# Reordering filler blocks, transposes and scores inside the attention slots of a global-local attention and routed-MLP kernel

## The chip, the cores and the metric

The kernel runs on one core of one Trainium2 chip. TensorE (PE) multiplies matrices into PSUM; VectorE (DVE) and ScalarE (ACT) read PSUM and work on SBUF; GpSimd (POOL) works on SBUF; POOL, ACT and SyncE (SP) issue DMAs. The metric is the time of one execution on the device in microseconds (us); lower is better. Several runs are taken and the median is given.

## The reference: what is computed

Two stages. The first is attention for 8 batches, 8 heads, 512 local and 32 global tokens of 64 values. Local tokens attend to the 32 global keys and to local keys no more than 32 places away; global tokens attend to all 544 keys.

```python
s_g = scale * np.matmul(q_g, k_all.transpose(0, 1, 3, 2))
out_g = np.matmul(sm(s_g), v_all)
mask = np.abs(pos[:, None] - pos[None, :]) <= window
s_ll = np.where(mask, scale * np.matmul(q_l, k_l.transpose(0, 1, 3, 2)), -1000000000.0)
s_l = np.concatenate([s_lg, s_ll], axis=-1)
out_l = np.matmul(sm(s_l), np.concatenate([v_g, v_l], axis=2))
```

The 4352 x 512 result `x` goes through 8 experts that are all evaluated and weighted by a matrix P, made by eight rounds of row and column scaling:

```python
for e in range(E):
    h = np.maximum(x @ w1[e], 0.0)
    out += P[:, e:e + 1] * (h @ w2[e])
```

## The kernel before

The order of instructions on each engine is the order in which the program text emits them; each engine works through its own list in order, and semaphores hold an instruction until its inputs and its buffer are ready.

The attention part runs in slots. Slot `s` belongs to a pair of heads of one batch (32 pairs, 4 per batch). It works on two pairs at once: it makes the scores of pair `s` and finishes pair `s-1`. The steps, by function and profile line:

- `st_B(s, part)`: scores on PE (L301 against local keys, L303 against global keys) for three, three and two blocks of 64 queries; for each block DVE applies mask and maximum (L308, tile `ms`) and ACT the exponential with its sum (L311, tile `Pu`).
- `st_N(s)`: DVE takes reciprocals (L347) and normalises the local probabilities in two pieces, six blocks and two (L348); POOL normalises the part that belongs to global keys, shared by all queries (L352, tile `Pl`).
- `st_D1(s-1)`: eight PE transposes of the local probabilities (L359, tile `ptw`) and their copy to SBUF on DVE (L361, `pw`).
- `st_D2(s-1)`: two PE transposes of the shared ones (L367) and their copy on ACT (L369, `pg`).
- `st_A(s+1)`: eight PE transposes of keys and queries of the next pair (L275), copied by DVE (L276, `kTe`) and ACT (L285, `qbd`).
- `st_E(s-1)`: the outputs of the local queries (L380, L383), copied by ACT (L386; by DVE for pairs 4 to 7).
- Global queries are taken for two pairs at a time. `st_G0` gathers them on POOL (L399). `st_G1`, at the end of odd slots from the ninth on, makes their scores on PE (L409), the maximum on DVE (L411, L412) and the exponential on ACT (L414, `Pg`). In the slot after, `st_GN` normalises on DVE (L420, L421), `st_G2` makes five PE transposes (L428) and a copy on ACT (L430, `pgs`, one buffer), and `st_G3` the outputs on PE (L442, L443), copied by ACT (L447).

PSUM pools set part of the order: `ps_tr` has two buffers for all transposes, `ps_sc` two for scores and global outputs, `ps_po` one, shared by `st_E` and `st_G1`, and `ps_mm` two for fillers and logits.

A filler block fills PE between these steps: `p_l1` makes 128 rows of a hidden layer of one of the first four experts for one batch, with four matmuls of 512 columns (L468) into a `ps_mm` buffer. Its ReLU, which empties the buffer, is done by ACT (L471) or DVE (L473); every eighth block stores a finished tile (L475). `f1("av")` emits two blocks, the first emptied by ACT ("a"), the second by DVE ("v"). There are 288 blocks. Before the change slots 9 to 32 emit seven blocks (odd) or eight (even); those left at the end of the loop are emitted between the rounds of the scaling of P. Every fourth slot from 5 on also emits the routing logits (L455).

In slots from the ninth on, the order of PE's work before the change is: local transposes, two fillers, first scores, shared transposes, global transposes (even slots, and slot 9), second scores, two fillers, key and query transposes, third scores, a filler, outputs, global outputs (even slots, and slot 9), two fillers, then one more filler in even slots, and the logits and global scores where the slot has them. After the loop come the scaling rounds with the remaining fillers, and a long stage of the other experts and all second layers (L821, L839, L932).

In the code `s` is the slot, `HP` is 4, `NU` is 32, `g1` says that the slot ends with global scores, `g23` that the slot before it did.

Of the kernel before, what the change touches and what calls it, by code (L numbers as in the profile page):

```python
# [23 lines left out]
def kernel(  # L24
# [26 lines left out]
    HP = H // 2  # L51
# [40 lines left out]
    with tc.tile_pool(name="att_c", bufs=1) as att_c, \  # L92
# [106 lines left out]
        def cast_g(f, g):  # L199
            t = att_in.tile([P, NJ, 4, Dh], FP16, tag="gs", name="gs", bufs=3)  # L200
            r = B * GP
            nc.gpsimd.tensor_copy(out=t[0:r], in_=f[0:r, 4 * g : 4 * g + 4].rearrange("p h (s d) -> p s h d", s=NJ))
            return t
# [83 lines left out]
        def st_B(n, part):  # L287
            b, hp = divmod(n, HP)
            qb, kt = qbd[n % 2], kTe[n % NK]
            if part == 0:  # L290
                st[n] = dict(Pu=att_wk.tile([P, NHB, SW], FP16, tag="Pu", name="Pu"),
                             mx=att_wk.tile([P, NHB], FP32, tag="mx", name="mx"),
                             sm=att_wk.tile([P, NHB], FP32, tag="sm", name="sm"))
            d = st[n]
            i0 = 3 * part
            ni = min(3, NHB - i0)
            sc = ps_sc.tile([P, 512], FP32, tag="sc")
            ms = att_wk.tile([P, 3, SW], FP32, tag="ms")
            for ii in range(ni):
                i = i0 + ii  # L300
                nc.tensor.matmul(sc[:, SW * ii : SW * ii + KW], qb[:, i, :],  # L301
                                 kt[:, HB * i : HB * i + KW], start=True, stop=True)
                nc.tensor.matmul(sc[:, SW * ii + KW : SW * (ii + 1)], qb[:, i, :],  # L303
                                 kgT[:, hp, Sg * b : Sg * (b + 1)], start=True, stop=True)
            for ii in range(ni):
                i = i0 + ii
                mi = 0 if i == 0 else (2 if i == NHB - 1 else 1)
                nc.vector.tensor_tensor_reduce(  # L308
                    out=ms[:, ii, :], in0=sc[:, SW * ii : SW * (ii + 1)], in1=mask[:, mi, :],
                    scale=-scale, scalar=BIG, op0=ALU.add, op1=ALU.min, accum_out=d["mx"][:, i : i + 1])  # L310
                nc.scalar.activation(out=d["Pu"][:, i, :], in_=ms[:, ii, :], func=AF.Exp, scale=-1.0,  # L311
                                     bias=d["mx"][:, i : i + 1], accum_out=d["sm"][:, i : i + 1])
# [42 lines left out]
        def st_D1(n):  # L355
            d = st[n]
            ptw = ps_tr.tile([P, NHB, P], FP16, tag="tr")
            for i in range(NHB):
                nc.tensor.transpose(ptw[:, i, :], d["Pu"][:, i, 0:KW], identity)  # L359
            d["pw"] = att_wk.tile([P, NHB, P], FP16, tag="pw", name="pw")  # L360
            nc.vector.tensor_copy(out=d["pw"], in_=ptw)  # L361

        def st_D2(n):
            d = st[n]
            pt = ps_tr.tile([P, 2, P], FP16, tag="tr")
            for t in range(2):
                nc.tensor.transpose(pt[:, t, :], d["Pl"][:, 4 * t : 4 * t + 4, :], identity)  # L367
            d["pg"] = att_wk.tile([P, 2, P], FP16, tag="pg", name="pg")
            nc.scalar.copy(out=d["pg"], in_=pt)  # L369
# [53 lines left out]
        def st_G2(b, g):  # L423
            Pg = gs[(b, g)][0]
            pt = ps_tr.tile([P, 5, P], FP16, tag="tr")
            for t in range(5):
                c0 = P * t if t < 4 else S - P
                nc.tensor.transpose(pt[:, t, :], Pg[:, c0 : c0 + P], identity)  # L428
            pgs = att_wk.tile([P, 5, P], FP16, tag="pgs", bufs=1)
            nc.scalar.copy(out=pgs, in_=pt)  # L430
            gs[(b, g)] = pgs
# [29 lines left out]
        def p_l1(e, m, fm, eng, pool=None, tag="mm"):  # L461
            n = groups[m][1]
            if fm == 0:
                hTs[(e, m)] = hpool.tile([P, FT, n], FP16, tag="hT", name="hT")
            hT = hTs[(e, m)]
            ph = (pool or ps_mm).tile([P, 512], FP32, tag=tag, name="ph")
            for dk in range(DP):
                nc.tensor.matmul(ph[:, 0:n], wts[e][:, dk, P * fm : P * (fm + 1)], xT[m][:, dk, :],  # L468
                                 start=(dk == 0), stop=(dk == DP - 1))
            if eng == "a":  # L470
                nc.scalar.activation(out=hT[:, fm, 0:n], in_=ph[:, 0:n], func=AF.Relu)  # L471
            else:
                nc.vector.tensor_scalar(out=hT[:, fm, 0:n], in0=ph[:, 0:n], scalar1=0.0, scalar2=None, op0=ALU.max)  # L473
            if fm == FT - 1:
                (nc.scalar if pool else nc.sync).dma_start(out=hd[e][m], in_=hT)  # L475
# [14 lines left out]
        def f1(engs, **kw):  # L490
            nonlocal n1
            v = 0
            for eng in engs:
                k, fm = divmod(n1, FT)
                if k < len(fill) and slot >= HP * fill[k][1] + 5:
                    p_l1(*fill[k], fm, eng, **kw)
                    n1 += 1
                    v += 1 if fill[k][1] < B else 0.5
            return v
# [88 lines left out]
        for s in range(HP, NU + 1):  # L588
            slot = s
            b, hp = divmod(s, HP)  # L590
            g1 = s in gat
            g23 = s - 1 in gat
            if g1:
                gn = divmod(gat[s], 2)
            if g23:
                gp = divmod(gat[s - 1], 2)
            if s == HP:
                st_A(s + 1)
                st_B(s, 2)
                st_E(s - 1)  # L600
                st_N(s, 0, 6)
                st_N(s, 6, NHB)
                select_v(1, 0, (0, 1))
                st_B(s + 1, 0)
                select_v(1, 0, (2, 3))
                select_v(1, 1, (NJ - 1,))
                slot = s + 1
                va, vb = vab[1]
                nc.scalar.dma_start(out=vb[0:HB, 0 : NJ - 1], in_=va[HB:P, 0 : NJ - 1])
                nc.scalar.dma_start(out=vb[HB:P, 0 : NJ - 1], in_=va[0:HB, 1:NJ])  # L610
                cast_qk(1, 1, gq)
                gcast = [(cast_g(x[0], x[1]), x) for x in ((kgf, 1, kgT), (qgf, 0, qgT), (qgf, 1, qgT))]
                load_w1e(3)
            else:
                if HP + 1 < s <= 2 * HP:
                    st_B(s, 0)
                st_D1(s - 1)
                if g23:
                    st_GN(*gp)
            if g1 and s > HP + 1:  # L620
                st_G0(*gn)
            f1("aa")
            if 2 * HP < s < NU:
                st_B(s, 0)
            if s > HP:
                st_D2(s - 1)
            if g23:
                st_G2(*gp)
            if HP < s < NU:
                st_B(s, 1)  # L630
            if s > HP:
                f1("va")
            if HP < s < NU - 1:
                st_A(s + 1)
            if HP < s < NU:
                st_B(s, 2)
            if s > HP:
                f1("v")
                st_E(s - 1)
            if s == HP + 1:  # L640
                for t, (src, g, dst) in gcast:
                    transpose_g(t, g, dst)
                st_G0(*gn)
            if g23:
                st_G3(*gp)
            if s > HP:
                f1("va")
            if HP < s < NU:
                st_N(s, 0, 6)
                st_N(s, 6, NHB)  # L650
            if s > 2 * HP and not g1:
                f1("v")
            if s >= 5 and (s - 5) % HP == 0:
                logits(NJ * ((s - 5) // HP), NJ)
            if g1:
                st_G1(*gn)
            if s < NU and b + 1 < B:
                if hp == 0:
                    load_qk(b + 1, 0, (nc.sync, nc.sync))
                    load_qk(b + 1, 1, (nc.sync, nc.sync))  # L660
                elif hp == 1:
                    cast_qk(b + 1, 0, gq)
                    if b >= NL - 1:
                        load_w1d(b + 1)
                elif hp == 2:
                    vq = load_v(b + 1)
                    run(vq[:3])
                    cast_qk(b + 1, 1, gq)
                else:
                    run(vq[3:])  # L670
# [408 lines left out]
    for i, (m, e) in enumerate(units):  # L1079
# [9 lines left out]
        elif i % 2 == 0:  # L1089
# [45 lines left out]
            else:  # L1135
                n = groups[m][1]
                h = hs[i + 1]
                s = ss[i + 1] = xsp.tile([P, HF, n], FP16, tag="xs", name="sl")
# [96 lines left out]
```

## Time and profile before

| | us |
|---|---|
| median of three runs | 1045.23 (1043.06 to 1045.32) |
| the profiled execution, its time | 1043.48 |
| the profiled execution, its span | 1041.5 |
| PE busy | 1012.5 (97%) |
| DVE busy | 895.7 (86%) |
| ACT busy | 525.2 (50%) |
| the chain that ended last: share of PE | 79% |

The span runs from the first to the last instruction of the profiled execution. Busy time of PE counts a matmul until its modelled end, while the next one has begun, so short waits of PE are seen better in the starts of the timeline than in its busy share. In the view of waits a line reads: the instruction that waited, what it waited for, microseconds in total, how often, and the longest. In the timeline a line is start, length, engine, line of the kernel, operation, tiles, shape and how many were merged into it; idle time before it stands in brackets.

### The profile page before, as it was taken

The page shows a single profiled execution, that of the slowest core. Times are in us where ns is not written, and L with a number is a line of the kernel's source. Part 1 is how long each engine was busy: PE and PEld are TensorE (multiplying, and loading weights), DVE is VectorE, ACT ScalarE, POOL GpSimd, SP SyncE. Part 2 cuts the span into 40 slices and gives each one's busy share as a digit, 9 for nine tenths or more (in the row PEclk, how much of TensorE's full clock was granted, in tenths as well). Part 3 has the DMA queues.
Part 4 walks back from the last instruction along what each step waited for, and adds up shares of the span by engine and source line. Part 5 has one row for each costly group of instructions (what it writes and reads, how often), then busy time and mean ns, then how long its engine had stood idle before and what let it go on. Part 6 is the DMA issues. An engine that isn't in the chain of part 4 may idle for free.

```text
span 1041.5 us, 23189 instructions
## 1 busy us (share of the span) xinstructions
PE 1012.5 (97%) x9286; PEld 740.6 (71%) x9286; DVE 895.7 (86%) x1748; ACT 525.2 (50%) x1320; POOL 146.2 (14%) x237
## 2 busy tenths in 40 slices
PE   7899999999999999999999999999999999999998
PEld 4555555555555466777778878878878878878887
DVE  8687777777776786999898999999999999999986
ACT  7777888787876665223223333334334333333331
POOL 7441423424312102001100000000000000000000
PEclk9899999999999999999999999999999999999999
DMA  9887588989945989936866646556555555645651
GB/s 273 183 219 206 117 269 180 221 234 185 246 144 135 276 258 321 289 102 214 312 252 228 221 143 232 189 177 227 195 180 185 210 175 209 216 172 180 210 191 28
DMA packets 103499, 213.72 MB, mean 205 GB/s; under 512 B 34192, under 2 KB 68448, under 8 KB 92896
## 3 DMA queue, kind: packets, MB, share of 16 engines
q1 hardware_dynamic: 56928, 167.47, 46.3%
q0 software_dynamic: 43856, 35.14, 18.7%
q10 hardware_dynamic: 2608, 9.64, 2.4%
q8 instruction: 73, 1.20, 0.4%
q14 instruction: 34, 0.28, 0.1%
HBM read 174.41 MB, written 59.12 MB: 224 GB/s over the span
## 4 chain that ended last, share of the span: by engine, by line
PE 79%; DVE 10%; ACT 6%; issue 2%; DMA 1%; SPq 0%; POOL 0%; ACTq 0%; DVEq 0%
PE m L932 26%; PE ph L468 15%; PE pf L839 10%; PE pm L932 10%; PE ph L821 10%; ACT Pu L311 3%; DVE Pu L348 3%; DVE h L689 2%; PE ptw L359 1%; DVE s L689 1%; ACT hT L471 1%; PE pt L275 1%; ACT qbd L285 1%; DVE o L948 1%; PE po L380 1%
## 5 line engine op out<-in xcount | busy, mean ns | idle before, releaser
L468 PE MATMUL ph<-xT,w1e 128*128 128x512 f16 (+1 forms) x1152 | 255.9, 367 | 0.2
L932 PEld LDWEIGHTS <-h 128*128 128x128 f16 x2160 | 210.0, 98 | 35.7 <-DVE h L689 2.2
L932 PE MATMUL m<-w2c,s 128*128 128x256 f16 x1620 | 199.9, 273 | 0.0
L932 PEld LDWEIGHTS <-s 128*128 128x128 f16 x1620 | 158.2, 98 | 27.0
L468 PEld LDWEIGHTS <-w1e 128*128 128x128 f16 x1152 | 105.3, 98 | 96.1 <-issue 3.0
L689 DVE TENSOR_TENSOR h<-h,pb 128x2048 f16<-128x2048 f16 (+2 forms) x66 | 155.0, 2348 | 1.8 <-DMA h<-hd 1.8
L823 ACT ACTIVATE h<-ph 128x512 f16<-128x512 f32 (+1 forms) x144 | 78.9, 550 | 151.6 <-PE ph L821 149.7
L846 ACT ACTIVATE h<-pf 128x512 f16<-128x512 f32 x144 | 82.9, 596 | 123.0 <-PE pf L839 103.7
L689 DVE TENSOR_TENSOR s<-h 128x1024 f16<-128x1024 f16 (+2 forms) x178 | 127.6, 758 | 14.8 <-ACT h L823 7.9
L932 PE MATMUL m<-w2c,h 128*128 128x256 f16 x1080 | 138.2, 273 | 0.0
L471 ACT ACTIVATE hT<-ph 128x512 f16<-128x512 f32 (+1 forms) x192 | 104.4, 559 | 47.5 <-PE ph L468 45.2
L821 PE MATMUL ph<-xs,w1s 128*128 128x512 f16 (+1 forms) x576 | 127.3, 355 | 1.0 <-DMA w1s<-w1d 1.0
L932 PE MATMUL pm<-w2c,h 128*128 128x256 f16 x1080 | 124.8, 273 | 0.5
L839 PEld LDWEIGHTS <-w1q 128*128 128x128 f16 x1008 | 98.5, 98 | 12.0
L311 ACT ACTIVATE Pu<-ms,mx 128x160 f16<-128x160 f32 x224 | 93.6, 421 | 5.1 <-DVE mx L308 2.6
L473 DVE TENSOR_SCALAR hT<-ph 128x512 f16<-128x512 f32 x96 | 66.1, 688 | 31.3 <-PE ph L468 30.6
L689 DVE TENSOR_TENSOR h<-h 128x1024 f16<-128x1024 f16 (+1 forms) x178 | 91.6, 556 | 0.4
L689 DVE TENSOR_TENSOR xs<-xg,pb 128x1024 f16<-128x1024 f16 (+2 forms) x48 | 79.7, 1661 | 7.6 <-ACT hT L471 7.6
L821 PEld LDWEIGHTS <-w1s 128*128 128x128 f16 x576 | 56.3, 98 | 38.9 <-DMA w1s<-w1d 1.3
L839 PE MATMUL pf<-xs,w1q 128*128 128x256 f16 x576 | 80.5, 272 | 0.0
L951 POOL DMA_DIRECT2D out_dram<-o x8 | 6.1, 757 | 530.1 <-DVE o L948 530.1
L308 DVE CUSTOM_DVE_ANT_0 ms<-sc,mask 128x160 f32<-128x160 f32 x224 | 59.9, 320 | 18.9 <-PE sc L303 18.3
(168 smaller groups left out, 1257.5 us busy)
## 6 DMA issues: line engine op xcount, KB each, us to landing
h<-hd SPq DMA_DIRECT2D x32, 1024.0 KB
w1q<-w1c SPq DMA_DIRECT2D x36, 896.0 KB
hd<-hT SPq DMA_DIRECT2D x26, 1024.0 KB
w1s<-w1d SPq DMA_DIRECT2D x18, 1024.0 KB
pb<-pd SPq DMA_DIRECT2D x64, 256.0 KB
w2c<-in_moe_w_dram POOLq DMA_DIRECT2D x16, 512.0 KB, 23.0
out_dram<-o POOLq DMA_DIRECT2D x8, 1024.0 KB, 4.7
f<-in_q_l_dram SPq DMA_DIRECT2D x15, 512.0 KB
```

The source lines that it names most:

```text
L308: nc.vector.tensor_tensor_reduce(out=ms[:, ii, :], in0=sc[:, SW * ii : SW * (ii + 1)], in1=mask[:, mi, :], scale=-scale, scalar=BIG, op0=A ...
L311: nc.scalar.activation(out=d["Pu"][:, i, :], in_=ms[:, ii, :], func=AF.Exp, scale=-1.0, bias=d["mx"][:, i : i + 1], accum_out=d["sm"][:, i ...
L348: nc.vector.tensor_tensor(out=d["Pu"][:, i0:i1, 0:KW], in0=d["Pu"][:, i0:i1, 0:KW], in1=d["rs"][:, i0:i1].unsqueeze(2).to_broadcast([P, i1 ...
L468: nc.tensor.matmul(ph[:, 0:n], wts[e][:, dk, P * fm : P * (fm + 1)], xT[m][:, dk, :], start=(dk == 0), stop=(dk == DP - 1))
L471: nc.scalar.activation(out=hT[:, fm, 0:n], in_=ph[:, 0:n], func=AF.Relu)
L473: nc.vector.tensor_scalar(out=hT[:, fm, 0:n], in0=ph[:, 0:n], scalar1=0.0, scalar2=None, op0=ALU.max)
L689: nc.vector.tensor_tensor(out=out, in0=in0, in1=in1, op=op)
L821: nc.tensor.matmul(ph[:, 0:n], w1s[i][:, dk, P * fm : P * (fm + 1)], xss[i][:, dk, 0:n], start=(dk == 0), stop=(dk == DP - 1))
L823: nc.scalar.activation(out=hs[i][:, fm, 0:n], in_=ph[:, 0:n], func=AF.Relu)
L839: nc.tensor.matmul(bank[:, 256 * c : 256 * (c + 1)], self.w[:, self.sta[q], k, P * c : P * (c + 1)], self.mov[q][:, k], start=(first and c ...
L846: nc.scalar.activation(out=self.h[:, k : k + 2, 256 * c : 256 * (c + 1)], in_=bank.rearrange("p (k t) -> p k t", k=2), func=AF.Relu)
L932: nc.tensor.matmul(pm[:, HD * t : HD * (t + 1)], lhs[0][:, k, lhs[1] + P * t : lhs[1] + P * (t + 1)], w[:, k, q - 1, :], start=(k == 0 and ...
```

## The change

From the ninth slot on (`s > 2 * HP`) four things move within a slot. One of the two fillers after the local transposes is emitted ahead of them. The shared transposes are emitted ahead of the first scores instead of behind them. The global transposes are emitted behind the second scores and the two fillers that follow. The last filler of an even slot is emptied by ACT and not by DVE. In slots with global outputs, whatever their number, the second of the two fillers after the second scores is emptied by DVE and not by ACT; this holds in slots 6 to 8 too.

```diff
+                if s > 2 * HP:
+                    f1("a")
                 st_D1(s - 1)
                 if g23:
                     st_GN(*gp)
             if g1 and s > HP + 1:
                 st_G0(*gn)
-            f1("aa")
+            f1("a" if s > 2 * HP else "aa")
+            if s > HP:
+                st_D2(s - 1)
             if 2 * HP < s < NU:
                 st_B(s, 0)
-            if s > HP:
-                st_D2(s - 1)
-            if g23:
+            if g23 and s <= 2 * HP:
                 st_G2(*gp)
             if HP < s < NU:
                 st_B(s, 1)
             if s > HP:
-                f1("va")
+                f1("vv" if g23 else "va")
+            if g23 and s > 2 * HP:
+                st_G2(*gp)
...
             if s > 2 * HP and not g1:
-                f1("v")
+                f1("a")
```

## The prediction

> **What bounds the kernel now.** I read the page first (its time is 1043.48 us, the span 1041.5), then the stage that the diff touches by windows, then its waits, then the timeline of PE, ACT and DVE around two slots.
>
> ```profile
> span 1041.5 us, 23189 instructions
> PE 1012.5 (97%) x9286; PEld 740.6 (71%) x9286; DVE 895.7 (86%) x1748; ACT 525.2 (50%) x1320; POOL 146.2 (14%) x237
> ```
> ```profile
> 26.00:52.00 26.00, 22.01 (x279) 14.33 (x277) 16.27 (x59) 18.66 (x62) 11.30 (x13) 0.80 0.84 184
> 93.00:330.00 237.00, 230.57 (x2556) 130.13 (x2556) 181.41 (x641) 192.41 (x610) 73.34 (x127) 1.00 0.78 201
> ```
> ```profile
> PEld L359 <- DVE Pu L348: 9.2, 24, 0.6
> PEld L428 <- DVE Pg L421: 2.6, 7, 0.4
> PE sg L409 <- ACT xT L386: 2.3, 5, 0.5
> ```
> ```profile
> 152.36 2.83 PE L468 MATMUL ph<-xT,w1e 128*128 128x512 f16 x12
> 155.26 0.89 PE L359 MATMUL ptw<-identity,Pu 128*128 128x128 f16 x8
> 156.00 1.89 PE L468 MATMUL ph<-xT,w1e 128*128 128x512 f16 x8
> ...
> 162.24 1.90 PE L468 MATMUL ph<-xT,w1e 128*128 128x512 f16 x8
> 164.59 0.61 PE L409 MATMUL sg<-kTe,qgbd 128*128 128x480 f16 x4 [0.45 <-ACT xT L386]
> ```
> ```profile
> 153.84 0.59 ACT L386 CAST xT<-po 128x512 f16<-128x512 f32 x1
> 154.32 0.42 ACT L447 CAST xT<-pog 64x64 f16<-64x64 f32 x2
> 154.77 0.60 ACT L471 ACTIVATE hT<-ph 128x512 f16<-128x512 f32 x1
> ...
> 166.55 0.71 ACT L414 ACTIVATE Pg<-sg,m 128x544 f16<-128x544 f32 x1 [1.51 <-DVE m L412]
> ...
> 167.25 1.08 ACT L471 ACTIVATE hT<-ph 128x512 f16<-128x512 f32 x2
> ```
> ```profile
> 154.25 0.96 DVE L348 TENSOR_TENSOR Pu<-Pu,rs 128x768 f16<-128x768 f16 x1
> ...
> 155.32 0.42 DVE L348 TENSOR_TENSOR Pu<-Pu,rs 128x256 f16<-128x256 f16 x1
> ```
>
> PE is the bound: 97%, and its modelled ends hide the rest, so I go by starts. One filler block (four 512-column matmuls) takes 0.86 us: the two from 156.00 are done at 157.72, where scores begin. Slots 9 to 32 run from 92.9 to about 340, 10.3 us each, and PE issues without a break except at a few places that recur. Columns of the windows are busy time of PE, PEld, DVE, ACT, POOL, then the granted clock and the DMA share.
>
> **Each part and its price.** I count what PE loses at each place, from a start minus the end of the issue before it.
>
> Filler ahead of the local transposes (L359). They wait for the normalised probabilities, 155.21 and 155.74 on DVE. In slot 15 the three blocks from 152.36 issue until 155.03 (the third waits 0.08 for an eviction), the transposes start at 155.26, and the next block at 156.00: eight transposes cost 0.44 elsewhere (key transposes, 149.87 to 150.31), so 0.23 + 0.30 is lost. In even slots it is 0.07 + 0.22 (165.15 to 165.81). Slots 11 to 31 odd: 11 x 0.53; 10 to 30 even: 11 x 0.29; slots 9 and 32 lose 0.97 and 0.89. Sum 10.9 us. A block of 0.86 reaches past 155.74 in each, so all goes. Queued behind the waiting filler are the transposes, their copy, and nothing on DVE that waits earlier.
>
> What is late next: that filler needs the PSUM buffer of the filler two before it (two buffers), evicted by ACT at 154.77 to 155.37. If ACT kept its times, PE, free at 155.03, would wait 0.39 in odd slots. But in even slots ACT loses one eviction between its exponentials and L386 ("va" becomes "vv", 0.50, half of the pair's 1.08 less overlap) and the pg copy (0.25 of its pitch) moves ahead of them, while scores come later after the slot's first filler. I set the rows of an even slot end to end in the new order, t = 0 at the first filler: Pg's exponential, eviction 2.30 to 2.89, second 2.80 to 3.39, pg copy to 3.65, six exponentials (0.415 each) from 3.55 to 6.05, pgs copy 6.04 to 6.73, two qbd copies to 7.80, two exponentials to 8.64, L386 8.63 to 9.22, two casts to 9.53, eviction 9.54 to 10.13. PE meanwhile: filler, transposes 0.86, filler 1.29, shared ones 2.15, scores 2.26, 2.50, two fillers from 2.94, global ones 4.67, keys 4.96, scores 5.40, filler 5.56, outputs 6.42, 7.04, three fillers to 10.11. The next head filler waits until 10.18: 0.07. Ends 0.07 and 0.39; I take 0.15, nearest to the laid-out rows: 11 x 0.15 = 1.7.
>
> Also new: the third filler of an even slot needs the head filler's buffer. Its eviction stands on ACT behind Pg's exponential (L414, whose input chain hangs on DVE, not on PE): 167.25 to 167.84 in the rows, while PE arrives by 2.74 after its slot's start at 165.08, at 167.82, or 0.14 earlier by the next item. Ends 0.07 and 0.39 (the same wait doubled is about that); I take 0.25: 11 x 0.25 = 2.8.
>
> Shared transposes (L367) ahead of scores. No stall of theirs is in the rows; their input is done on POOL at 166.10 and they now come at 167.2, so the cover is 1.1 us. The gain is on ACT: the pg copy leaves the stretch that ends in L386. In odd slots L386 ends at 164.54 and L409 starts at 164.59, where PE was free at 163.97: 0.62 lost, 0.16 in slots with logits. The same laying-out for an odd slot puts L386 at 8.12 to 8.71 with PE free at 8.28: 0.48. Gain 0.14 x 11 = 1.5; ends 0 and 0.25 (the whole pg pitch).
>
> Global transposes (L428) behind second scores and two fillers. They lose 0.39 and 0.11 in alternate even slots waiting for L421 (slot 14: 147.22 to 147.61), 0.36 in slot 32; sum 3.1, and all goes, since two blocks and scores (1.96) pass first. Late next is L430's copy (ends 6.73) and L442, which wants it at 7.04: 0.26 of cover after 0.05 for the hand-over.
>
> Evictions. "vv" also holds in slots 6 to 8, which the change's heading does not name. There the key copy on DVE (65.98) would come about 0.2 later behind a second eviction, and ACT's qbd copies wait for it (0.09 in the rows), so exponentials and the following transposes slip: 3 x 0.2 = 0.6 lost; the ends are 1.5 won (the 0.50 that ACT is freed of, three times) and 1.5 lost. The last filler's eviction from DVE to ACT ("v" to "a") frees DVE's transpose copy, which nothing waits for early. The number of blocks, of evictions on each engine and of DMAs is the same, and the order of SP's and POOL's instructions is unchanged, so eighth-block stores keep their place; 208 filler blocks are gone by the loop's end in both, and the tail is the same work, starting earlier.
>
> Sum: removed 10.9 + 3.1 + 1.5 = 15.5; added 1.7 + 2.8 + 0.6 = 5.1; net 10.4 us. 1043.48 - 10.4 = 1033.1. The runs' median is 1045.23, 1.75 above the profiled one; I put the median after at 1034.0.
>
> **Rivals.**
>
> The wait only changes its name. ACT has few gaps from its first exponential to L386, so fillers wait for evictions where transposes waited for DVE. Then per pair of slots 0.82 + 0.25 is won, 0.39 + 0.39 lost, L409 unchanged: 0.3 to 0.4, with slots 9 and 32 some 5 us: 1039.5. For it: ACT is 0.39 late at 155.37. Against: an eviction less on ACT there. 14%.
>
> Loads set the pace. DMA share is 0.85 to 0.91 in four-slot windows, and a share of 1.00 stands between 339 and 400. If loads kept the old pace the gain returns as stalls: 1044. Against: in 93 to 330 no PE wait names a DMA, and between 298 and 330 the share is 0.33, so nothing is owed when the tail begins. 5%.
>
> Slower: the pgs copy. It now stands behind six exponentials and the global outputs (L442) wait for it in every even slot. Each 0.1 that it ends later than laid out, past 0.26, costs 12 x 0.1; the net gain of 10.4 is gone when it ends 1.1 us late. If it also fell behind the qbd pair and two exponentials (1.16 + 0.83 = 2.0), L442 would wait 1.74, 12 x 1.74 = 20.9: 1054. For it: ACT goes in order and one pgs buffer exists. Against: it is issued ahead of the qbd pair. 7%.
>
> Slower: the clock. From 26 to 52 us the granted clock is 0.80, so this core can lose it; the loop's issue time of some 228 us at 0.80 would be 57 longer: about 1091. Against: 1.00 in all of 93 to 330, where third fillers wait 0.08 on the two buffers already. 1%. [...]
>
> **Chances and range.** A difference under 0.3% (3.1 us) can't be told from none here. Forecast, 1034.0, own range 1030.5 to 1037.5: 73%; renamed wait 14%; loads 5%; slower 8%. Ends of the unknown waits: all at their best the gain is 10.4 + 0.9 + 2.0 + 1.2 + 2.1 = 16.6, at their worst 10.4 - 2.6 - 1.5 - 1.5 - 0.9 = 3.9. With the renamed wait in, 1030 to 1041. Faster 0.86, same 0.06, slower 0.08.
>
> **What would show it.** Right: no wait of L359 for L348 and none of L428 for L421 in slots 9 to 32; slots of about 9.8 us instead of 10.26; the fourth filler in a row 0.1 to 0.2 late in odd slots, the third of an even slot 0.2 late behind L414; L409 still waiting near 0.5 for L386. Wrong: L442 waiting for L430, L471 evictions that hold every head filler 0.4 or more, a clock under 1.00, or an end of the loop that comes earlier while the tail's first loads do not.

## The result and the profile after

The changed kernel takes 1033.81 us (median of four runs, 1033.11 to 1034.16) where the kernel before takes 1045.20 (1043.06 to 1045.32, four runs, one more than in the table above): a ratio of 0.9895, 95% interval 0.9878 to 0.9912. The profiled execution took 1033.45 us. The head of its page:

```profile
span 1031.3 us, 23197 instructions
PE 1004.4 (97%) x9286; PEld 739.9 (72%) x9286; DVE 896.5 (87%) x1752; ACT 521.6 (51%) x1316; POOL 146.3 (14%) x237
```

PE still bounds the kernel with the same 9286 matmuls. Its waits in the slots, from the view of waits of the changed kernel between 91 and 330 us (who waited for whom, us in total, times, longest):

```profile
DVE pw L361 <- PE ptw L359: 11.1, 12, 1.0
PE sg L409 <- ACT xT L386: 1.7, 5, 0.6
PE ph L468 <- ACT hT L471: 1.3, 2, 0.9
```

The lines of L359 for L348 and of L428 for L421 are gone. The relation of the local transposes has turned round: now DVE's copy (L361) waits for PE. What is left on PE are L409, as before, and a new wait of fillers for evictions on ACT. The two waits in its line are those of slots 9 and 32; in the other slots it is mostly too short for the view, and it is read in the starts. PE and ACT of the changed kernel around slots 14 to 16:

```profile
142.12 1.03 PE L468 MATMUL ph<-xT,w1e 128*128 128x512 f16 x4
142.99 0.28 PE L367 MATMUL pt<-identity,Pl 128*128 128x128 f16 x2
143.84 1.89 PE L468 MATMUL ph<-xT,w1e 128*128 128x512 f16 x8
145.57 0.44 PE L428 MATMUL pt<-identity,Pg 128*128 128x128 f16 x5
...
148.34 3.89 PE L468 MATMUL ph<-xT,w1e 128*128 128x512 f16 x16
152.07 0.61 PE L359 MATMUL ptw<-identity,Pu 128*128 128x128 f16 x8
152.51 1.03 PE L468 MATMUL ph<-xT,w1e 128*128 128x512 f16 x4
...
160.09 0.61 PE L409 MATMUL sg<-kTe,qgbd 128*128 128x480 f16 x4 [0.29 <-ACT xT L386]
```
```profile
142.50 0.71 ACT L414 ACTIVATE Pg<-sg,m 128x544 f16<-128x544 f32 x1 [1.76 <-DVE m L412]
143.21 1.07 ACT L471 ACTIVATE hT<-ph 128x512 f16<-128x512 f32 x2
...
150.56 1.25 ACT L471 ACTIVATE hT<-ph 128x512 f16<-128x512 f32 x2
```

The transposes at 152.07 take 0.44 us to the next filler at 152.51; before it was 0.74 in this slot. The four fillers from 148.34, the last of them the filler that is now emitted ahead of the transposes (the head filler), are through at 152.07, 3.73 us where issue alone takes 3.45: 0.08 for an eviction on DVE as before, and 0.20 for the head filler, whose buffer ACT empties by about 151.15. The pair of evictions at 143.21 stands behind L414; the first ends about 143.80, and the third filler of the slot starts at 143.84, 0.26 after PE was free. The global transposes (145.57) follow the two fillers without a gap. Slots 14 to 29 take 9.86 us each, before 10.27 (the prediction had 9.8 from 10.26).

To compare runs I take one stretch, called the stage below: from the last L409 of slot 8 to the first matmul of the scaling of P. In the changed kernel these are:

```profile
90.65 0.20 PE L409 MATMUL sg<-kgT,qgbd 128*128 128x32 f16 x2
331.54 0.38 PE L988 MATMUL pm<-dg,ones_f 128*128 128x128 f32 x2
```

The second of the two L409 starts at 90.68, so the stage is 240.9 us; in the profile before it ran from 92.21 to 342.21, 250.0 us. The stage thus gave 9.1 of the 10.2 us between the two spans. Another 1.5 came ahead of it: the first filler starts at 45.04 us instead of 46.56, before any code that the change touches. The tail took 0.5 longer (699.7 against 699.3; in all fourteen profiles it lies between 699.1 and 700.0). The 1.5 goes with the granted clock of the early part, which was 0.80 before (the prediction shows the line) and is 0.93 in the changed kernel; the last section tells how far that explains it. In the windows view the clock is the third number from the end:

```profile
26.00:52.00 26.00, 20.93 (x293) 14.18 (x292) 17.02 (x61) 19.68 (x65) 10.93 (x13) 0.93 0.87 188
91.00:330.00 239.00, 234.57 (x2664) 135.53 (x2663) 186.01 (x656) 195.39 (x620) 79.08 (x134) 1.00 0.82 206
```

### The profile page after: what moved, and what is told of

Read it like the earlier page. It is cut to its first block, busy times and chain, and to the rows that moved or that the text cites. A ratio compares the mean times of both kernels' runs of the same rounds, so it can differ in the third digit from the quotient of the medians.

```text
span 1031.3 us, 23197 instructions
## 1 busy us (share of the span) xinstructions
PE 1004.4 (97%) x9286; PEld 739.9 (72%) x9286; DVE 896.5 (87%) x1752; ACT 521.6 (51%) x1316; POOL 146.3 (14%) x237
## 4 chain that ended last, share of the span: by engine, by line
PE 79%; DVE 9%; ACT 6%; issue 3%; DMA 2%; POOL 0%; SPq 0%; ACTq 0%; DVEq 0%; POOLq 0%
PE m L936 25%; PE ph L468 18%; PE pf L843 10%; PE pm L936 10%; PE ph L825 9%; ACT Pu L311 2%; DVE Pu L348 2%; DVE h L693 1%; PE pt L275 1%; ACT qbd L285 1%; DVE s L693 1%; DVE o L952 1%; PE ptw L359 1%; PE po L380 1%; ACT hT L471 1%
## 5 line engine op out<-in xcount | busy, mean ns | idle before, releaser
L468 PE MATMUL ph<-xT,w1e 128*128 128x512 f16 (+1 forms) x1152 | 259.8, 367 | 2.6 <-ACT hT L471 1.3
L471 ACT ACTIVATE hT<-ph 128x512 f16<-128x512 f32 (+1 forms) x188 | 102.0, 558 | 38.2 <-PE ph L468 35.2
L473 DVE TENSOR_SCALAR hT<-ph 128x512 f16<-128x512 f32 x100 | 67.7, 687 | 28.1 <-PE ph L468 28.0
```

## The experiments

Theory A: the waits hang on one chain. ACT, from its first exponential to the copy of the outputs, and DVE's normalisation behind it leave PE so much and no more; a part of the change that removes one wait exposes the next, so parts win little alone and lose much when taken away. Theory B: each part wins the stall that the profile of before shows at its place, and the wins add up.

| kernel | median, us | ratio to before, interval | stage, us |
|---|---|---|---|
| before | 1045.20; 1043.34 to 1044.38 beside the runs below | 1 | 250.0 |
| the change | 1033.81 | 0.9895, 0.9878 to 0.9912 | 240.9 |
| no head filler | 1039.66 | 0.9956, 0.9941 to 0.9971 | 246.9 |
| no eviction moved to DVE | 1039.67 | 0.9955, 0.9940 to 0.9970 | 246.4 |
| shared transposes not moved | 1035.07 | 0.9913, 0.9896 to 0.9929 | 242.6 |
| global transposes not moved | 1038.38 | 0.9945, 0.9931 to 0.9960 | 245.2 |
| last eviction not moved to ACT | 1034.31 | 0.9912, 0.9897 to 0.9927 | 241.0 |
| head filler alone | 1041.51 | 0.9977, 0.9968 to 0.9987 | 248.5 |
| no second DVE eviction in slots 6 to 8 | 1032.99 | 0.9901, 0.9887 to 0.9916 | 240.9 |
| two waits more removed | 1031.81 | 0.9881, 0.9865 to 0.9898 | 238.0 |
| the same again | 1031.89 | 0.9885, 0.9870 to 0.9901 | 238.0 |
| head filler of even slots on DVE | 1033.36 | 0.9898, 0.9882 to 0.9915 | 239.9 |
| both: two waits more removed, and all head fillers of even slots on DVE | 1027.79 | 0.9851, 0.9834 to 0.9868 | 235.7 |
| the change again | 1033.97 | 0.9907, 0.9892 to 0.9921 | 240.8 |

The last four stand beside each other on one chip. The stage is the finer measure: it came out at 240.86 and 240.83 us in the two profiles of the changed kernel, and at 237.97 and 237.96 in the two with two waits more removed. Medians that differ by about 1 us or less belong to runs whose ranges overlap, so such differences are read from the stage alone.

**No head filler.**

```diff
-                if s > 2 * HP:
-                    f1("a")
                 st_D1(s - 1)
...
-            f1("a" if s > 2 * HP else "aa")
+            f1("aa")
```

> All of the change but the head filler: both fillers stand behind the local transposes again. Stage time is taken in the profile from the end of slot 8's global scores (L409) to the first scaling round's matmul; before 250.0 us, changed kernel 240.8. Theory A (the parts hang on one chain; a part can only win what ACT and DVE leave free): with the head filler gone the transposes wait for the normalisation again, 0.5 us in odd slots, 0.4 in even ones, and the stage is back at 248.7, nearly all gain lost. Theory B (each part wins its own stall and the wins add up): the head filler's own part is 10.9 less the waits it brought (some 4.5), so the stage is 247.2 at most and the total about 1040.

Stage 246.9 us. The view of waits has the old line back:

```profile
PEld L359 <- DVE Pu L348: 9.6, 27, 0.6
```

By the starts the transposes lose 0.52 in odd slots, as before, and 0.40 to 0.43 in most even ones, where it was 0.26. Over all slots they lose 11.7 us again, and the fillers wait 5.7 less. Taking the head filler away thus costs 6.0 us. The place is as A said, but the size is B's: 246.9 lies under B's 247.2, and A's 248.7 is 1.8 too much. This run alone would speak for B.

**The head filler alone.**

```diff
+                if s > 2 * HP:
+                    f1("a")
                 st_D1(s - 1)
...
-            f1("aa")
+            f1("a" if s > 2 * HP else "aa")
```

> The head filler alone, nothing else of the change. Theory A: stage 248.2 us (before 250.0): the local transposes no longer wait, but the head filler waits 0.36 in odd slots for an eviction on ACT, and the global transposes 0.40 to 0.50 for L421 in even ones. Theory B: 10.9 less 4.5, stage 243.6, total about 1039.

Stage 248.5 us, as A said (248.2), and B's 243.6 is refuted: alone the part wins 1.5 us, in company 6.0, so the wins do not add up. Its starts on PE show where the 10.4 us of removed waits went:

```profile
146.18 0.27 PE L367 MATMUL pt<-identity,Pl 128*128 128x128 f16 x2
146.95 0.45 PE L428 MATMUL pt<-identity,Pg 128*128 128x128 f16 x5 [0.50 <-DVE Pg L421]
...
151.70 2.83 PE L468 MATMUL ph<-xT,w1e 128*128 128x512 f16 x12
154.75 1.02 PE L468 MATMUL ph<-xT,w1e 128*128 128x512 f16 x4 [0.21 <-ACT hT L471]
```

Two shared transposes take 0.11, so L428 comes 0.66 late in this slot (0.39 in the next even one, against 0.39 and 0.11 before), and the fourth filler in a row 0.38 late (three take 2.59 from 151.70, and 0.08 goes to the third). In sum the global transposes wait 7.6 us instead of 3.1, and the head fillers 4.5.

**No eviction moved to DVE.**

```diff
-                f1("vv" if g23 else "va")
+                f1("va")
```

> All of the change but the eviction that moved from ACT to DVE in slots with global outputs. Theory A: ACT is the limit between its first exponential and the copy of the outputs, so 0.5 us more on it in each even slot comes back as waits of PE: head filler of odd slots 0.33 (0.20 in the changed kernel), global outputs L442 0.24 behind the copy L430 in even slots; stage 246.5 us, 5.7 more than the changed kernel. Theory B: it only rebalances, its stall was none, stage 240.8.

The edit also takes the second DVE eviction out of slots 6 to 8, which alone does nothing (see below). Stage 246.4 us: one eviction of 0.5 us of ACT's time per even slot costs 5.5 us, though PE's work is the same. That the total is A's 246.5 is luck: of its two places the head filler waits more than A said, 0.62 instead of 0.33 in odd slots from the thirteenth on, and the global outputs less, 0.08 instead of 0.24. The head filler:

```profile
153.47 1.09 ACT L471 ACTIVATE hT<-ph 128x512 f16<-128x512 f32 x2
154.12 1.02 PE L468 MATMUL ph<-xT,w1e 128*128 128x512 f16 x4 [0.46 <-ACT hT L471]
```

The global outputs wait for L430 to end: their gap is 0.18 where it is 0.10 in the changed kernel. This is the mechanism of the prediction's slower rival, at 0.08 us, in a kernel that gives ACT half a microsecond more.

**Global transposes not moved.**

```diff
-            if g23 and s <= 2 * HP:
+            if g23:
                 st_G2(*gp)
...
-            if g23 and s > 2 * HP:
-                st_G2(*gp)
```

> All of the change but the global transposes, which stand ahead of the second scores again. Theory A: the filler ahead has moved PE's work earlier and Pg no earlier, so they wait 0.55 in every even slot for L421 (before: 0.39 and 0.11), and the third filler's wait of 0.2 goes in return; stage 244.3 us. Theory B: the stalls of before come back, 3.1 us, stage 243.9, with waits of 0.39 and 0.11.

Stage 245.2 us. L428 waits 0.54 and 0.80 in alternate even slots; in the view of waits:

```profile
PEld L428 <- DVE Pg L421: 8.8, 13, 1.2
PE pt L428 <- DVE Pg L421: 6.9, 12, 1.1
```

The wait is longer than before the change, as A said, by more than A said. The third filler's wait is gone in return.

**Shared transposes not moved.**

```diff
-            if s > HP:
-                st_D2(s - 1)
             if 2 * HP < s < NU:
                 st_B(s, 0)
+            if s > HP:
+                st_D2(s - 1)
```

> All of the change but the shared transposes, which stand behind the first scores again. Theory A: the copy L369 is back between the exponentials; L409 waits 0.62 in odd slots without logits and key transposes wait 0.1 for the copy's buffer; stage 242.4 us. Theory B: its own part is 0.14 in 11 slots, 1.5 us, stage 242.3: here both say the same, and the place tells: A wants a wait of key transposes for L369, B none.

Stage 242.6 us. L409 waits 0.62 again, and key transposes of even slots wait 0.04 or 0.21, the place that A alone named.

**Last eviction of even slots not moved.**

```diff
             if s > 2 * HP and not g1:
-                f1("a")
+                f1("v")
```

> All of the change but the last filler of even slots, which DVE empties again. Both theories: DVE's copy of the local transposes comes later and nothing on PE wants it early; stage 240.9 us against 240.8, no difference in the total. A rival: that ACT runs short in even slots, and an eviction back on DVE wins 1 us or more.

Stage 241.0 us: this part does nothing for the time in this company, and the rival that ACT would be better without it falls.

**No second DVE eviction in slots 6 to 8.**

```diff
-                f1("vv" if g23 else "va")
+                f1("vv" if g23 and s > 2 * HP else "va")
```

> The change with the second DVE eviction left out in slots 6 to 8 alone. The prediction had charged 0.6 us for it there. If that was right, this is 0.6 us faster in slots 6 to 9; if the key copy's delay and ACT's freed 0.5 us cancel, it is the same within 0.1, seen in the starts of slots 7, 8 and 9.

Slots 6 to 8 take 32.88 us, with the eviction 32.87, and before 32.87. The key copy does come later (the changed kernel, DVE; 1.53 us are to be added for the early part to compare it with 65.98 of before):

```profile
64.61 0.68 DVE L276 COPY kTe<-pt 128x512 f16<-128x512 f16 x1
65.70 0.69 DVE L473 TENSOR_SCALAR hT<-ph 128x512 f16<-128x512 f32 x1
67.37 0.69 DVE L473 TENSOR_SCALAR hT<-ph 128x512 f16<-128x512 f32 x1 [0.39 <-PE ph L468]
67.97 0.18 DVE L347 RECIPROCAL rs<-sm 128x6 f32<-128x6 f32 x1
```

That is 0.16 later. But the reciprocal (L347) stands on DVE behind a filler's eviction, which itself waits for PE, and starts 1.53 earlier than the 69.50 of before, like everything around it. The exponentials' delay ends in front of that eviction.

**What the third filler of an even slot waits for.**

```diff
                 if s > 2 * HP:
-                    f1("a")
+                    f1("v" if s > 2 * HP + 1 and g23 else "a")
```

> The change, with the head filler of even slots (from slot 10 on) emptied by DVE. It tells what the third filler of even slots waits for. If it is ACT's place behind the exponential of the global scores (L414), its wait of 0.19 and 0.26 is gone; the eviction is then missing on ACT, so nothing is won elsewhere, and DVE's later evictions give fillers of even slots 0.1: stage 238 to 241 us (changed kernel 240.9). If it is the head filler's late start, the wait stays. Slot 32's wait of 1.1 goes in the first case.

Its wait is gone in every even slot, slot 32's falls from 1.11 to 0.32: it was the place behind L414. The stage is 239.9, only 0.9 less, since the head filler of odd slots now waits 0.29 to 0.45 instead of 0.20. I had not named that place; why ACT comes later there was not tested.

**Two waits more removed, and all three.** The first kernel lets DVE copy the local outputs in even slots (`n` odd) and empty slot 32's head filler:

```diff
                 if s > 2 * HP:
-                    f1("a")
+                    f1("v" if s == NU else "a")
...
-            cp = nc.vector.tensor_copy if HP <= n < 2 * HP else nc.scalar.copy
+            cp = nc.vector.tensor_copy if HP <= n < 2 * HP or (n > 2 * HP and n % 2 == 1) else nc.scalar.copy
```

> The change, with DVE copying the local outputs in even slots (L386) and emptying slot 32's head filler. Theory A: the head filler of odd slots finds its buffer (0.20 to 0), and slot 32's third filler loses most of its 1.1; stage 239.3 us, 1.5 less than the changed kernel, total 1032.3. Rival: DVE's copy stands ahead of the reciprocals and delays the normalisation, so waits come back at the transposes: 241 or more.

> The same kernel as in the run with DVE copying the local outputs in even slots and emptying slot 32's head filler, beside the changed kernel on one chip: 1.5 to 2.9 us below it, stage 238.0.

Stage 238.0 us in both runs. The head filler's 0.20 is gone and slot 32's wait is 0.32: 2.1 in the eleven odd slots and 0.79 make 2.9, the whole difference. On one chip its median is 2.1 us below that of the change. The second kernel empties every even slot's head filler on DVE instead, beside that copy:

> Both: DVE copies the local outputs in even slots, and DVE empties the head filler of every even slot from 10 on. If the two waits (head filler of odd slots behind ACT, third filler of even slots behind L414) are separate, both are gone and the stage is 236 to 237 us, total 1030; if DVE is then the late one (two evictions, the copy and the normalisation in one slot), fillers or transposes wait for DVE and the stage is 238 or more.

> The changed kernel itself, for a comparison on one chip: about 10 us below the kernel before, stage 240.9.

Stage 235.7 us, 1027.79 us, against 1033.97 of the change on the same chip. Separately the two edits take 2.9 and 0.9 off the stage, together 5.2. In its starts four fillers in a row go 0.19 faster than in the changed kernel, and the pair after the scores follows them at once:

```profile
141.67 1.03 PE L468 MATMUL ph<-xT,w1e 128*128 128x512 f16 x4
142.53 0.28 PE L367 MATMUL pt<-identity,Pl 128*128 128x128 f16 x2
143.13 1.89 PE L468 MATMUL ph<-xT,w1e 128*128 128x512 f16 x8
...
147.63 3.70 PE L468 MATMUL ph<-xT,w1e 128*128 128x512 f16 x16
151.16 0.61 PE L359 MATMUL ptw<-identity,Pu 128*128 128x128 f16 x8
```

That is more than their sum, since the copy on DVE also removes the longer wait of the head filler that the other edit alone brings. What is left are mainly waits of L409 (0.46 in five slots), the third fillers of slot 9 (0.55) and slot 32 (0.32), and 0.08 behind DVE.

## Why the prediction was right, point by point

| step | predicted, us | measured, us |
|---|---|---|
| local transposes | 10.9 won | 10.4 won (0.1 stays in slot 9) |
| global transposes | 3.1 won | 3.2 won |
| L409 | 1.5 won | 1.4 won |
| head fillers | 1.7 lost | 2.2 lost (0.20 in ten odd slots, 0.10 in one, 0.15 in slot 10) |
| third fillers, even slots | 2.8 lost | 2.1 lost (0.26 and 0.19 in turn from slot 14 on, 0.10 in slot 10, none in slot 12) |
| slots 6 to 8 | 0.6 lost | 0 |
| slots 9, 31 and 32 | not named | 1.8 lost |
| not placed | | 0.2 won |
| net in the stage and before it | 10.4 | 9.1 |

The mechanism was right. The waits removed were counted from the profile, 15.5 us, and came out at 15.0; the local transposes were counted somewhat high, since an even slot had lost 0.26 and not 0.29. For L409 the sum is right and its parts are not all as said: slots 15, 19, 23 and 27 gain 0.16 each and slots with logits 0.10 to 0.14, while slot 11 waits 0.11 longer. The new waits came where the rows, laid end to end in the new order, had put them, and their sizes lay between the named ends in nearly all middle slots. How near the chosen 0.15 and 0.25 came to the measured 0.20, 0.26 and 0.19 is partly luck, since they were picked between 0.07 and 0.39; the head fillers' sum was 0.5 too small and the third fillers' 0.7 too large, which nearly cancel.

Two steps were off. The sum took 11 middle slots for the new waits of fillers and left out the ends of the loop:

```profile
94.11 1.89 PE L468 MATMUL ph<-xT,w1e 128*128 128x512 f16 x8 [0.39 <-ACT hT L471]
321.37 1.89 PE L468 MATMUL ph<-xT,w1e 128*128 128x512 f16 x8 [0.94 <-ACT hT L471]
```

By the starts the third filler loses 0.55 in slot 9 and 1.11 in slot 32. In both, Pg's exponential starts 2.1 us after the last global score and not 1.7 as in slot 14 (L414 at 92.77, 320.03 and 142.50; L409 at 90.68, 317.92 and 140.77), and in slot 32 no scores stand between the transposes and the third filler. In slot 31 the filler ahead of the outputs waits 0.11 more, for an eviction on DVE (L473 ends at 314.09, the filler starts at 314.14). And the charge for slots 6 to 8 was for a delay that is absorbed behind a filler's eviction on DVE. The chain of copies that I followed was real, but I did not look at what stands just ahead of the reciprocal.

The net of the stage was therefore 9.1 and not 10.4. The predicted 1034.0 is as close to 1033.81 as it is partly by chance: the part ahead of slot 9 gave 1.5 us that have nothing to do with the change, and the tail took 0.5 back. The later comparison on one chip, 1033.97 to 1043.34, is 9.4 apart, near the stage's own 9.1.

The rivals: the renamed wait is real: the fillers' new waits are 2.2, 2.1 and, in slots 9 and 32, 1.7 us, four tenths of the 15.0 removed, and with the head filler alone the new waits eat nearly all. Loads held nothing back: the DMA share rose from 0.78 to 0.82 in the slots and no wait of PE names a load. The pgs copy held nothing in the changed kernel (L442 starts 0.10 after the local outputs, as before). The clock stayed at 1.00 from 91 to 330 us, with four fillers in a row on two PSUM buffers.

What the prediction did not say is how the parts hang together. Taken away one at a time they cost 6.0, 5.5, 4.3, 1.7 and 0.1 us, 17.6 in sum, where all together are worth 9.1.

## What to carry to other kernels

When an engine in order waits at a few fixed places of a loop, list them with their sizes, move the work, and then lay the rows of the engine that feeds it end to end in the new order: here that gave the places of the next waits in the middle slots, and bounds for their sizes. Do the same for the first and last turns of the loop, where the work between two dependent steps is shorter. Parts of such a reordering are not worth the stall they name; test them by taking each away as well as alone, and look for the next gain where the remaining waits name one queue, here ACT's evictions and copies moved to DVE.

## What was not expected of the hardware

The time ahead of slot 9 differs from profile to profile by up to 3.1 us with nearly the same instructions there. By the granted clock between 26 and 52 us the fourteen profiles fall into four groups:

| granted clock, 26 to 52 us | profiles | the part ahead of slot 9 ends at, us |
|---|---|---|
| 0.93 | 5 | 90.51 to 91.73 |
| 0.87 | 3 | 90.89 to 91.78 |
| 0.80 | 4 | 91.82 to 92.21 |
| 0.74 | 2 | 92.83 and 93.62 |

A lower clock goes with a later end, but up to 1.2 us remain between profiles of one clock, and no run separates whether the clock makes the delay. The 3.1 us are 0.3% of the kernel, about what separates its runs (1042.41 to 1045.61 in thirteen runs of the kernel before), and have to be taken out before two single profiles of this kernel are compared to a microsecond. In the changed kernel the clock is 0.50 from 33.88 to 37.29 us, a stretch of 3.41 us, and 1.00 in the rest of the 26. In the kernel before it is 0.50 from 33.12 to 43.36 us, 10.24 us and three times as long, and 1.00 in the rest. If the other two groups lose it at 0.50 as well, their 0.87 and 0.74 come to 6.8 and 13.5 us, an estimate from those means alone.

The second unexpected thing is how much one eviction of 0.5 us is worth. ACT is busy 195.39 of 239 us in the slots, 82%, and still an eviction per even slot moved from it to DVE brought 5.5 us: it stands in the stretch of ACT ahead of the eviction that PE waits for, and without the move the head filler of odd slots waits 0.62 us and not 0.20.
